# Top-32 attention and a low-rank mixer: first batch's last steps masked at once on VectorE, weight rounding with sign bits from ScalarE

## The chip, the cores and the metric

One core of one Trainium2 chip runs the whole program: one launch, all inputs and outputs in the chip's memory. The metric is the device time of one execution in microseconds. Times of a kernel are medians over several executions; the profile is one more execution, with its own time. The profile's "span" runs from the first to the last recorded instruction of that execution.

Five engines matter. TensorE (PE, with PEld for its weight loads) multiplies matrices and transposes tiles through an identity matrix. VectorE (DVE) finds maxima and masks. ScalarE (ACT) evaluates exponentials, scaled copies and rectifications. GpSimd (POOL) does elementwise work. SyncE (SP) issues transfers. Each works through its own list of instructions in order and waits on semaphores for the others.

## The reference

Attention with a top-32 mask per row feeds a mixer. All sizes are fixed: 8 batches, 8 heads, 576 positions, head size 64.

```
scores = scale * q @ k.T                    # (8, 8, 576, 576)
kth    = 32nd largest score of each row
scores = where(scores >= kth, scores, -1e9)
attn   = exp(scores - rowmax)
attn   = attn / (sum(attn) + 1e-9)
x      = (attn @ v), heads side by side     # (8, 576, 512)

u   = x + (x.T @ U @ V).T                   # U: 576x32, V: 32x576
out = u + relu(u @ w_ch1) @ w_ch2           # w_ch1: 512x2048, w_ch2: 2048x512
```

The four parameters U, V, w_ch1 and w_ch2 come in as 64-bit floats and q, k, v as 32-bit floats. The kernel reads each 64-bit number as two 32-bit words and builds the nearest 32-bit float from them with integer arithmetic.

## The kernel before

**Steps.** Heads are taken in pairs: 4 pairs a batch, 32 in all (g). The rows of a pair are cut into four blocks of 128 rows and one of 64 (t = 0 to 4). One pass of the main loop, with counter n and `g, t = divmod(n, 5)`, is called step n here; there are 160 steps, 20 for each batch. At t = 4 both heads' 64 rows share one tile of 128 rows, so such a step has half the work. Step 18 is the last full block of batch 0, and step 19 is its last half block.

**Inside a step.** `scores` multiplies q by k for a block (L271) and ScalarE copies the result to the tile Ssb (L290 to L292, L281). `front` works on VectorE: the eight largest of each row (MAX8, L317), then three rounds of striking these out (MATCH_REPLACE8, L325) and finding the next eight (L329). The smallest of the fourth eight is the threshold. ScalarE's `nmax` (L321) prepares the row maximum and `weigh` (L297) takes the exponential. The first head of a block is weighed early and then masked on VectorE by one SCALAR_TENSOR_TENSOR (L334) that also sums the row. The second head takes another way: after the threshold is known, GpSimd writes a large negative number where a score is too small (L332) and adds it to the scores (L333), and ScalarE takes the exponential after that, in the next step, summing as it goes. `front` is a Python generator: each `next(here)` writes out the instructions up to its next `yield`, and `next(last, None)` writes the late exponential of the step before.

`turns` transposes the weights block by block on TensorE (L361, L366) with ScalarE copies to PT (L362, L367). `values` multiplies PT with v (L390, L393, and L380 at t = 4), with copies to XT (L402) and at t = 4 the scaled copies to x (L388). At t = 4 it also writes the inverse of the row sums `den` (L377, L378) for all nine columns of the pair. `mixed` transposes XT back (L414), scales by the inverse on GpSimd (L419), multiplies with U (`pT`, L425, copy Tb L433) and V (`up`, L437 and L439) and stores u in uT (L447).

**Feed-forward part.** When a batch's four pairs are mixed, `mlp` becomes a stream of matmuls (L462 with copies hT L474, then L481, adds L497 and output turns L509) that `fill` deals out between the attention instructions in fixed portions. So batch b's feed-forward work runs beside batch b + 1's attention, and batch 7's runs alone at the end. During batch 0 there is nothing to deal out.

**The turn.** ALONE is 20: steps up to 20 are written out by a first branch of the loop and later ones by a second. In step 20 the first branch also finishes values of steps 18 and 19 and all of `mixed` for pair 3, so that the first L462 can follow.

**Rounding of parameters.** 36 groups of 64-bit words are loaded and rounded: four small ones for U and V, 16 blocks of w_ch1, 16 of w_ch2. `next_params(1)` is one turn of a three-stage pipeline: it joins the group that was converted at the previous call (`f64_join`), converts the one that was loaded at the previous call (`f64_parts`) and issues the load of a new one on SP's queue (512 KB for a weight block). The conversion is ScalarE's absolute value (L157), GpSimd's maximum with a tiny number (L158), ScalarE's scaling of the low word's top byte (L159) and ScalarE's sign (L160). The join is VectorE's shift left by three (L168), GpSimd's addition of the sign word (L169) and GpSimd's addition of the low word with its rounding (L171). It is called once a step, and a second time in steps 11 and 16 and, after step 20, where t is 1 or 3.

**Order.** Nothing reorders instructions on TensorE, ScalarE, VectorE and GpSimd: each does them in the order in which the Python code writes them out. So moving a call moves its instructions past everything between.

Of the kernel before, what the change touches and what calls it, by code (L numbers as in the profile page):

```python
# [8 lines left out]
F32 = mybir.dt.float32  # L9
U8 = mybir.dt.uint8  # L10
U32 = mybir.dt.uint32
AF = mybir.ActivationFunctionType
ALU = mybir.AluOpType
# [8 lines left out]
def kernel(  # L22
# [28 lines left out]
    nc = tc.nc  # L51
    B, H, S, D = q.shape
    P = 128
# [51 lines left out]
    V = const.tile([NT * R, S], F32, name="V")  # L105

    step = const.tile([P, 1], F32, name="step")
    nc.vector.memset(step, 2.0**23)
# [32 lines left out]
    def f64_parts(raw, out):  # L141

        n, w = raw.shape[0], raw.shape[-1] // 2
        d = "p f" if len(raw.shape) == 3 else "p"
        low, hi = (raw.rearrange(f"{d} (w two) -> {d} w two", two=2)[..., i] for i in range(2))
        low8 = raw.bitcast(U8).rearrange(f"{d} (w eight) -> {d} w eight", eight=8)[..., 3]
        if out is None:
            if not spare:  # L150

                uT = mlpp.tile([P, NC, S], F32, tag="uT", name="uT")
                words = uT.rearrange("p c n -> p (c n)").bitcast(U32)
                spare.extend(words[:, i * SLAB : (i + 1) * SLAB] for i in range(NT))
            out = spare.pop()[0:n, 0:w]
        bits = out.bitcast(U32)
        nc.scalar.activation(bits.bitcast(F32), hi.bitcast(F32), AF.Abs)  # L157
        nc.gpsimd.tensor_scalar(bits.bitcast(F32), bits.bitcast(F32), TINY, None, ALU.max)  # L158
        nc.scalar.activation(low, low8, AF.Identity, bias=step[0:n], scale=(1 + 2.0**-10) / 32)  # L159
        nc.scalar.activation(hi.bitcast(F32), hi.bitcast(F32), AF.Sign, bias=nudge[0:n])  # L160
        return hi, bits, low

    def f64_join(hi, bits, low, outs):

        nc.vector.tensor_single_scalar(bits, bits, 3, ALU.logical_shift_left)  # L168
        nc.gpsimd.tensor_tensor(bits, bits, hi, ALU.add)  # L169
        for dst, form in outs:  # L170
            nc.gpsimd.tensor_tensor(dst.bitcast(U32), form(bits), form(low), ALU.add)  # L171

# [126 lines left out]
    def front(g, t):  # L299
# [18 lines left out]
        yield  # L318
        for i in range(1, TOPK // 8):
            if i == 1:  # L320
                nc.scalar.mul(nmax[:, 0:n], first[:, 0:n, 0], -SCALE)  # L321
                weigh(chunks[0], Es[0], nmax[:, 0:1])
# [8 lines left out]
        if n == 2:  # L331
            nc.gpsimd.tensor_scalar(Es[1], chunks[1], ms[1][:, 7:8], NEG, ALU.is_lt, ALU.mult)  # L332
            nc.gpsimd.tensor_tensor(chunks[1], chunks[1], Es[1], ALU.add)  # L333
        nc.vector.scalar_tensor_tensor(  # L334
            out=Es[0],
            in0=chunks[0],
            scalar=ms[0][:, 7:8],
            in1=Es[0],
            op0=ALU.is_ge,
            op1=ALU.mult,  # L340
            accum_out=sums[0],
        )
# [3 lines left out]
        if n == 2:  # L346
            weigh(chunks[1], Es[1], nmax[:, 1:2], sums[1])
# [21 lines left out]

    def values(g, t):  # L370
# [4 lines left out]
        if t == NT:  # L375
            den, x = dens[g], xs[g % 2]
            nc.vector.tensor_scalar_add(den, den, 1e-9)  # L377
            nc.vector.reciprocal(den, den)  # L378
# [26 lines left out]
    def mixed(g, wait):  # L405
# [4 lines left out]
        XT, den = XTs.pop(g), dens.pop(g)  # L410
# [144 lines left out]
    t = 0  # L555
# [5 lines left out]
    for n in range(STEPS + 2):  # L561
# [9 lines left out]
        if n <= ALONE:  # L571
            next(turning, None)
            next(turning, None)
            if n < ALONE:
                scores(*divmod(n + 1, CH))
# [3 lines left out]
            if n == ALONE:  # L579

                next(turning)
                next(turning)
# [3 lines left out]
            if n == ALONE:  # L586
                values(*divmod(n - 1, CH))
                mixing.append(mixed((n - 1) // CH, 1))
                fill()
                scores(*divmod(n + 1, CH))  # L590
                while mixing:
                    fill()
            next_params(1)
            if n and n < ALONE:
                next(turning)
# [74 lines left out]
```

## Time and profile before

| what | value |
|---|---|
| median of 3 executions | 1872.28 us (1869.91 to 1872.94) |
| the profiled execution's own time | 1873.04 us |
| its span | 1871.2 us, 29270 instructions |
| PE busy | 1751.0 us, 94% |
| DVE busy | 1620.9 us, 87% |
| ACT busy | 1008.6 us, 54% |
| POOL busy | 690.8 us, 37% |

Busy time by stage, in microseconds, with TensorE's granted clock as a share of full speed:

| stage (us) | PE | DVE | ACT | POOL | clock |
|---|---|---|---|---|---|
| 0 to 240 | 143.33 | 225.44 | 140.23 | 148.17 | 0.71 |
| 240 to 355 | 103.94 | 104.82 | 81.47 | 97.41 | 1.00 |
| 355 to 1735 | 1372.93 | 1287.03 | 768.70 | 444.52 | 1.00 |
| 1735 to 1871 | 130.79 | 3.63 | 18.24 | 0.72 | 0.99 |

The first stage is batch 0's attention with the first 20 joins of parameters. In the second the feed-forward matmuls of batch 0 run beside batch 1's attention and the w_ch2 blocks are rounded. The third has no rounding left. The last is batch 7's feed-forward part alone.

In the listings that follow, a line of a timeline gives start and duration in microseconds, engine, line, operation, tiles written and read, and in brackets the engine's idle time before the instruction with what ended it. A line of the chain gives start, length and what the chain passed through: the chain is followed back from the last instruction, at each step to whatever released it.

### The profile page before, as it was taken

How to read it: one execution, taken by the hardware profiler on the slowest of the kernel's cores; microseconds unless marked ns; L12 is line 12 of the kernel's file. 1: busy time of each engine (PE TensorE's matmuls, PEld its weight loads, DVE VectorE, ACT ScalarE, POOL GpSimd, SP SyncE). 2: the span in 40 equal slices, each digit the busy share in tenths (PEclk: the TensorE clock that was granted, in tenths of full speed). 3: DMA queues.
4: the chain of work that ended last, by engine and by line, in shares of the span. 5: the costliest groups of instructions: out<-in, count | busy, mean ns of one | idle time of the engine just before them, and what ended most of it. 6: DMA issues, size and time to landing. Idle time of an engine off the chain costs nothing.

```text
span 1871.2 us, 29270 instructions
## 1 busy us (share of the span) xinstructions
PE 1751.0 (94%) x10528; PEld 1327.4 (71%) x10528; DVE 1620.9 (87%) x3312; ACT 1008.6 (54%) x2467; POOL 690.8 (37%) x470
## 2 busy tenths in 40 slices
PE   4566699999999999999999999999999999999999
PEld 3344466687677877788777877778777877778777
DVE  7999989999999999999999999999999999996000
ACT  4566576665555555555555556565655655554111
POOL 3667788633223332333323333333233232322000
PEclk7667699999999999999999999999999999999999
DMA  3222222110001010101001010010001010000000
GB/s 86 65 71 74 67 84 80 41 25 23 18 17 31 21 32 20 28 22 26 14 24 30 22 32 19 24 26 20 20 20 31 24 30 21 9 8 7 6 14 12
DMA packets 127296, 58.23 MB, mean 31 GB/s; under 512 B 89904, under 2 KB 124976, under 8 KB 127152
## 3 DMA queue, kind: packets, MB, share of 16 engines
q1 hardware_dynamic: 126096, 56.10, 11.1%
q8 instruction: 84, 1.38, 0.3%
q14 instruction: 60, 0.49, 0.1%
q10 hardware_dynamic: 1056, 0.26, 0.1%
HBM read 46.89 MB, written 9.44 MB: 30 GB/s over the span
## 4 chain that ended last, share of the span: by engine, by line
PE 85%; DVE 7%; ACT 5%; POOL 1%; issue 1%; DMA 0%; POOLq 0%; SPq 0%; DVEq 0%; ACTq 0%
PE mm L462 27%; PE mm L481 25%; PE sc L271 9%; PE O L393 7%; PE tp L361 6%; DVE rr L325 3%; DVE m L329 2%; PE up L437 2%; PE O L380 2%; PE O L390 2%; PE tp L251 1%; ACT E L297 1%; DVE first L317 1%; PE tp L509 1%; PE up L439 1%
## 5 line engine op out<-in xcount | busy, mean ns | idle before, releaser
L329 DVE MAX8 m<-rr 128x8 f32<-128x576 f32 x864 | 614.6, 748 | 5.3
L481 PE MATMUL mm<-hT,w 128*128 128x256 f32 (+1 forms) x2048 | 562.4, 410 | 0.0
L462 PE MATMUL mm<-uT,w 128*128 128x256 f32 (+1 forms) x2048 | 558.2, 411 | 1.5 <-ACT hT L474 1.5
L332 POOL TENSOR_SCALAR E<-Ssb,m 128x576 f32<-128x576 f32 x128 | 287.9, 2249 | 619.5 <-DVE m L329 495.2
L462 PEld LDWEIGHTS mm<-uT,w 128*128 128x128 f32 x2048 | 364.6, 191 | 107.9 <-issue 27.9
L481 PEld LDWEIGHTS mm<-hT,w 128*128 128x128 f32 x2048 | 361.3, 191 | 97.2 <-issue 22.5
L325 DVE MATCH_REPLACE8 rr<-m,rr 128x576 f32<-128x576 f32 x576 | 427.5, 742 | 0.0
L361 PE MATMUL tp<-ident,E 128*128 128x128 f32 x1152 | 185.3, 286 | 59.5 <-ACT E L297 42.1
L362 ACT COPY PT<-tp 128x512 f32<-128x512 f32 x288 | 168.1, 584 | 120.0 <-PE tp L361 118.1
L297 ACT ACTIVATE E<-Ssb,nmax 128x576 f32<-128x576 f32 x288 | 223.8, 777 | 7.6 <-POOL Ssb L333 2.4
L361 PEld LDWEIGHTS tp<-ident,E 128*128 128x128 f32 x1152 | 144.8, 147 | 112.8 <-ACT E L297 54.7
L271 PE MATMUL sc<-qkT 64*128 64x288 f32 (+1 forms) x1280 | 212.3, 453 | 0.2 <-ACT Ssb L292 0.2
L325 DVE MATCH_REPLACE8 rr<-first,Ssb 128x576 f32<-128x576 f32 x288 | 211.7, 742 | 0.0
L317 DVE MAX8 first<-Ssb 128x8 f32<-128x576 f32 x288 | 205.3, 749 | 0.9 <-ACT Ssb L292 0.9
L334 DVE SCALAR_TENSOR_TENSOR E<-Ssb,m,E 128x576 f32<-128x576 f32 x160 | 138.2, 864 | 63.2 <-ACT E L297 46.9
L333 POOL TENSOR_TENSOR Ssb<-Ssb,E 128x576 f32<-128x576 f32 x128 | 180.3, 1409 | 10.7
L474 ACT ACTIVATE hT<-mm 128x320 f32<-128x320 f32 (+1 forms) x256 | 104.2, 407 | 119.9 <-PE mm L462 119.1
L402 ACT COPY XT<-O 128x128 f32<-128x128 f32 x128 | 34.0, 266 | 213.6 <-PE O L393 213.6
L271 PEld LDWEIGHTS sc<-qkT 64*128 64x128 f32 (+1 forms) x1280 | 110.4, 187 | 51.6 <-issue 25.0
L393 PE MATMUL O<-PT,va 128*64 128x128 f32 x2048 | 146.3, 287 | 0.0
L494 DVE TENSOR_TENSOR oT<-uT,mm 128x320 f32<-128x320 f32 (+1 forms) x8 | 3.6, 454 | 146.6 <-PE mm L481 146.6
L393 PEld LDWEIGHTS O<-PT,va 128*64 128x64 f32 x2048 | 114.7, 142 | 16.4 <-issue 2.2
(75 smaller groups left out, 1543.0 us busy)
## 6 DMA issues: line engine op xcount, KB each, us to landing
raw<-in_moe_w_ch_dram SPq DMA_DIRECT2D x32, 512.0 KB, 3.7
va<-in_v_dram SPq DMA_DIRECT2D x64, 128.0 KB, 2.4
out_dram<-ob SPq DMA_DIRECT2D x64, 128.0 KB, 1.9
ld_q<-in_q_dram SPq DMA_DIRECT2D x63, 128.0 KB, 2.7
ld_k<-in_k_dram SPq DMA_DIRECT2D x63, 128.0 KB, 2.8
ld_ends<-in_q_dram SPq DMA_DIRECT2D x32, 32.0 KB, 2.1
ld_ends<-in_k_dram SPq DMA_DIRECT2D x32, 32.0 KB, 2.1
vd<-in_v_dram SPq DMA_DIRECT2D x64, 16.0 KB, 2.0
```

The lines of the kernel that those rows point to most:

```text
L271: nc.tensor.matmul(sc[slice(0, n) if t < NT else half(h), h, 0:HALF], lhsT=qkT[half(h), 0, cols(t)], rhs=qkT[half(h), 1, i * HALF : (i + 1 ...
L297: nc.scalar.activation(E, chunk, AF.Exp, bias=nmax, scale=SCALE, accum_out=total)
L317: nc.vector.max(ms[c], curs[c])
L325: nc.vector.match_replace(nxt, ms[c], curs[c], NEG)
L329: nc.vector.max(ms[c], curs[c])
L332: nc.gpsimd.tensor_scalar(Es[1], chunks[1], ms[1][:, 7:8], NEG, ALU.is_lt, ALU.mult)
L333: nc.gpsimd.tensor_tensor(chunks[1], chunks[1], Es[1], ALU.add)
L361: nc.tensor.transpose(tp[:, j, :], E2[:, a : a + P], ident)
L362: nc.scalar.copy(PT[:, NT * h : NT * h + NT], tp)
L393: nc.tensor.matmul(O[half(h)], lhsT=va[:, h, j, :], rhs=PT[:, NT * h + j], start=False, stop=(j == NT - 1),)
L462: nc.tensor.matmul(ph[:, 0:w], lhsT=w1[:, cc, f * P : (f + 1) * P], rhs=uT[:, cc, lo:hi], start=(cc == 0), stop=(cc == NC - 1),)
L481: nc.tensor.matmul(po[:, 0:w], lhsT=w2[:, f, c * P : (c + 1) * P], rhs=hTs[f][:, 0:w], start=(f == 0), stop=(f == NF - 1),)
```

## The change

It has three parts.

1. **Rounding.** The conversion gets a fourth ScalarE instruction: after the sign, Identity with scale 2^30 and bias -2^30, written as a 32-bit integer, turns +1 into 0 and -1 into the sign bit alone. The join's shift on VectorE and the sign's addition on GpSimd become one VectorE instruction with two tensor inputs (shift left by three, then exclusive or). The constants change to suit. For each of the 36 groups ScalarE has one instruction more, GpSimd one less, and VectorE's has one input more.
2. **Step 18.** Both heads are weighed early and masked on VectorE; nothing of this step goes to GpSimd.
3. **Steps 19 and 20.** They get a branch of their own. Step 19 writes out all remaining turns of step 17, the scores of step 20, all turns of step 18, the values of 17 and 18, the inverse of the first eight row sums and the first part of `mixed` for pair 3; it has no call of `next_params`. Step 20 writes out the turns and values of 19 (with the inverse of the ninth row sum), the multiplication with U, then the scores of 21 and the rest of `mixed`. The later parameter groups each move one call back.

```diff
-        nc.scalar.activation(low, low8, AF.Identity, bias=step[0:n], scale=(1 + 2.0**-10) / 32)
+        lows = low.bitcast(F32)
+        nc.scalar.activation(lows, low8, AF.Identity, bias=two[0:n], scale=(1 + 2.0**-10) * 2.0**-27)
         nc.scalar.activation(hi.bitcast(F32), hi.bitcast(F32), AF.Sign, bias=nudge[0:n])
+        nc.scalar.activation(hi.bitcast(I32), hi.bitcast(F32), AF.Identity, bias=less[0:n], scale=2.0**30)
         return hi, bits, low
...
-        nc.vector.tensor_single_scalar(bits, bits, 3, ALU.logical_shift_left)
-        nc.gpsimd.tensor_tensor(bits, bits, hi, ALU.add)
+        nc.vector.scalar_tensor_tensor(
+            out=bits, in0=bits, scalar=3, in1=hi, op0=ALU.logical_shift_left, op1=ALU.bitwise_xor
+        )
...
+        pooled = n == 2 and (g, t) != (NPAIR - 1, NT - 1)
...
-                weigh(chunks[0], Es[0], nmax[:, 0:1])
+                for c in range(1 if pooled else n):
+                    weigh(chunks[c], Es[c], nmax[:, c : c + 1])
...
-        if n == 2:
+        if pooled:
             nc.gpsimd.tensor_scalar(Es[1], chunks[1], ms[1][:, 7:8], NEG, ALU.is_lt, ALU.mult)
             nc.gpsimd.tensor_tensor(chunks[1], chunks[1], Es[1], ALU.add)
-        nc.vector.scalar_tensor_tensor(
+        for c in range(1 if pooled else n):
+            nc.vector.scalar_tensor_tensor(
...
-        if n == 2:
+        if pooled:
             weigh(chunks[1], Es[1], nmax[:, 1:2], sums[1])
...
+    def inverse(g, lo, hi):
+        den = dens[g][:, lo:hi]
+        nc.vector.tensor_scalar_add(den, den, 1e-9)
+        nc.vector.reciprocal(den, den)
...
-            nc.vector.tensor_scalar_add(den, den, 1e-9)
-            nc.vector.reciprocal(den, den)
+            inverse(g, 2 * NT if g == NPAIR - 1 else 0, 2 * NT + 1)
...
+        if n >= ALONE - 1 and n <= ALONE:
+
+            list(turning)
+            if n < ALONE:
+                scores(*divmod(n + 1, CH))
+            list(turns(*divmod(n - 1, CH)))
+            if n < ALONE:
+                values(*divmod(n - 2, CH))
+                next(here)
+            values(*divmod(n - 1, CH))
+            if n < ALONE:
+                inverse(g, 0, 2 * NT)
+                next(here)
+                mixing.append(mixed(g, 1))
+                fill()
+                next(here)
+                next(here)
+                continue
+            fill()
+            scores(*divmod(n + 1, CH))
+            next(here)
+            while mixing:
+                fill()
+            next_params(1)
+            fill()
+            next(last, None)
+            next(here)
+            fill()
+            next(here)
+            next(here)
+            fill()
+            continue
```

In the first branch of the loop, now for steps below 19 alone, the lines for step 20 are gone; the calls of the other steps stay as they were.

## The prediction

> **What bounds the kernel now.** I read the page first (slices, then the chain), then the chain, the engine timelines and the busy times for the first 480 us, which is where the change lies. Step n below is pass n of the main loop; E(n) is its score tile after the mask.
>
> The slices show two regimes. Up to about 240 us VectorE is at nine tenths and TensorE at half of a reduced clock; afterwards TensorE is full.
>
> ```profile
> PE   4566699999999999999999999999999999999999
> DVE  7999989999999999999999999999999999996000
> PEclk7667699999999999999999999999999999999999
> ```
>
> From 11 to 241 us VectorE has one gap (0.48 us at 217.42), so the attention steps 0 to 19 run at VectorE's pace. From 239 to 355 us the feed-forward matmuls of batch 0 run beside the steps, and there VectorE's share misleads. The chain for this stretch contains no VectorE piece. It alternates between TensorE and ScalarE, and the three weight-rounding instructions (L157, L159, L160) lie on it, ahead of the copies and the exponentials that TensorE waits for:
>
> ```profile
> 270.57 0.78 ACT E L297
> 271.35 0.57 ACT w L157
> 271.91 0.67 ACT raw L159
> 272.59 0.66 ACT raw L160
> 273.24 0.02 issue
> 273.27 0.44 ACT hT L474
> 273.70 0.48 ACT PT L362
> 274.18 0.76 ACT E L297 x2
> ```
>
> TensorE's timeline shows the matching gaps, in brackets with their releaser:
>
> ```profile
> 273.76 0.81 PE L462 MATMUL mm<-uT,w 128*128 128x320 f32 x2 [0.81 <-ACT hT L474]
> ...
> 285.43 0.66 PE L361 MATMUL tp<-ident,E 128*128 128x128 f32 x4 [1.54 <-ACT E L297]
> ...
> 332.15 0.66 PE L361 MATMUL tp<-ident,E 128*128 128x128 f32 x4 [1.80 <-ACT E L297]
> ```
>
> VectorE in the same stretch waits six times (8.4 us) for the rounding maximum on GpSimd; that is its slack against this loop. From 355 to the end TensorE has one larger gap (2.9 us at 470, behind GpSimd's mask of that step), so whatever the loop loses by 355 stays in the span.
>
> **The change, part by part.**
>
> *Rounding on VectorE.* L168 is one-input; its successor starts 0.33 us later (220.56 to 220.88). The two-input form has no row. Bounds: unchanged rate (+0) below; above, the mask L334, 0.82 us with its successor after 0.74, so +0.41. The nearest rows for 512 values at one per cycle are VectorE's copies L253 (512 values, 0.69) and L290 (576, 0.76); less the 0.07 by which neighbours overlap (a pair of maxima takes 1.41 for two of 0.75) that gives 0.62, so I take +0.30. Seventeen of the twenty joins up to step 18 have this width: 17 x 0.30 = 5.1, and 0.1 for the small ones.
>
> *GpSimd loses L169* (1.29 to 1.46 us, 36 times). What it gives VectorE is less collision:
>
> ```profile
> 204.03 1.76 DVE L334 SCALAR_TENSOR_TENSOR E<-Ssb,m,E 128x576 f32<-128x576 f32 x1
> 209.83 1.30 DVE L168 TENSOR_SCALAR w<-w 128x512 uint32<-128x512 uint32 x1
> 224.27 0.82 DVE L334 SCALAR_TENSOR_TENSOR E<-Ssb,m,E 128x576 f32<-128x576 f32 x1
> ```
>
> The first stood against GpSimd's L171 (203.89 to 205.18), the second against L333 (209.43 to 210.84), which was late behind the rounding. There are four such in stage one (148.86, 154.66, 204.03, 209.83), 0.88 to 0.94 each. I take 3.0 saved, with 0 and 3.6 as ends.
>
> The Trainium skill (SBUF — State Buffer, Who interferes with whom) says that a VectorE instruction with two SBUF inputs contends with any GpSimd instruction that reads SBUF, and that the later one fully blocks. The trace agrees for GpSimd's tensor-tensor but not for its tensor-scalar: the third line above took 0.82 with L158 running from 223.72 to 225.22. By the rule's wording a join that meets the 1.5 us L158 would wait too and the rounding would cost up to 1.5 us more at each meeting; by the row it costs nothing, and the sum goes by the row.
>
> *Step 18.* Its second head is masked on VectorE: +0.82 by L334. So E(18) ends 5.2 - 3.0 + 0.8 = 3.0 us later (ends: -2.8 and +7.9). Off GpSimd go 2.2 + 1.4 us (L332, L333).
>
> *The turn from step 18 to the feed-forward part.* Before, E(18)'s VectorE mask ended at 218.16, the second head came through GpSimd and a late exponential only at 225.0, and the first L462 started at 239.05: 20.9 us. After, I walk the changed kernel's order of instructions on TensorE. The scores of step 20 end 0.75 after E(18): they ended at 218.28 against 218.16, and ScalarE now has a second exponential (0.69) and a conversion (0.66) ahead of the one they wait behind, against the mask's 0.8 on the other side. Then transposes of 18: 2.4; values of 17 and 18: 2.6 each; wait and XT transposes 1.2; transposes of 19: 1.4; PT copy 0.6; values of 19: 2.4; L388 0.65; pT 0.7; scores of 21: 1.25; up 1.75. That is 18.3 us at the durations of this stage, whose clock is low. In the trace the clock came up after some 8 us without a gap (scores 2.29 us at 215.99, 1.24 at 234.46). TensorE now has fewer gaps, so it may come up from values(18) on, which takes 3.3 off: 15.0. I take the middle, 16.6. So L462 starts 3.0 - 4.3 = 1.3 us earlier than 239.05. The split inverse costs VectorE two small instructions in step 19 (0.15 and 0.21, the rows of L377 and L378 at 229.12), and the join dropped there gives back 0.33.
>
> *The added ScalarE conversion*, the one that decides. No row has it; the rows of the same width with a bias operand, L159 and L160, have pitches of 0.65 to 0.67. The ends are L157's 0.57 and L159's whole 0.77; I take 0.66, since form and bias are theirs. On a stretch where ScalarE runs without a gap from the score copies to the instruction TensorE waits for, it lengthens the loop by all of it. Before, fourteen conversions follow 239 us; after, fifteen, since step 19 no longer makes one and all later ones move one place back. Step by step: step 20, nothing (TensorE has 5.4 us of L462 queued); 21, 0.66 and 0.05 (its second conversion has 0.6 of cover before L390); 22, 0.66 (gap of 0.65 at 262.44); 23, twice 0.66 (gaps at 273.76 and 277.87); 24, 0.66; 25, 0.22 (hT has 0.43 of cover); 26, 0.4 (Tb waits for the two conversions, while pT gains from GpSimd's missing L169); 27, 0.66; 28, twice 0.66; 29, 0.66; 30, 0.15 (the displaced one, beside a TensorE that has no gap). Nine full ones are 5.9, the rest 0.8: 6.7 us. If only half bite: 3.4; if every one bites and the displaced one wholly (2.5): 12.
>
> The Trainium skill (ScalarE: Activation LUTs, Rules for kernel authors and What ACT_TABLE_LOAD costs) speaks against the move: additions and multiplications belong on VectorE. Its price for 512 values with a pointer bias is 0.28 + 0.43 - 0.09 = 0.61 us per successor, so 9 x 0.61 = 5.5 as an estimate by that page where the rows give 5.9.
>
> *Costed at nothing.* VectorE after 240 us: sixteen joins at +0.30 are 4.8, covered by the 8.4 us that it waits. If that cover goes, it sets the pace instead (rival two). The dropped call in step 19 also moves a 512 KB load one place back in SP's queue, behind the next pair's V; it lands in 3.7 us and is converted a step (some 11 us) later. The last weight block is joined in step 31 rather than 30, near 359; its first reader, a late L481 of that step, ran at 365.1. That leaves 6 us.
>
> **Sum.** -1.3 + 6.7 = +5.4 on the span: 1871.2 + 5.4 = 1876.6. The profiled execution took 1873.04, 1.84 more than its span: 1878.4. It was 0.76 above the median of 1872.28, so the forecast is 1877.7.
>
> **Rivals.**
> *One: the loop has more give than its gaps say.* For it: TensorE starts the loop some 4 us further ahead of VectorE, and waits that belong to VectorE leave room. Against: the brackets name ScalarE, which was itself without a gap. Half of the conversions bite and the clock comes up early: 3.0 - 5.9 + 3.4 = +0.5, 1872.8.
> *Two, faster: VectorE is the clock to 470 us*, as its 95% says, and the change frees it. Its waits of 8.4 go; collisions saved come to 5.0 over both stages; 33 joins cost 9.9 and the mask 0.8: -2.7, and the 0.8 that L334 waits at 443 goes too: 1868.8. It decides as soon as the loop's own path falls below that -3.5: if L462 starts 5 us earlier, say, and no more than two conversions bite. Against: no VectorE piece is in the chain from 239 to 443.
> *Three: dearer joins.* At +0.41 and with no collision saved, E(18) is 7.9 late, L462 starts 3.6 late, and the loop adds 6.7: +10.3, 1882.6. For it: the raw words are read with a stride. Against: GpSimd's L169 on the same stride takes 1.29, no more than its dense L333 (1.41 for 576).
>
> **How the numbers follow.** The forecast's case 0.55, rival one 0.23, rival two 0.11, rival three 0.11. The likeliest case's own range is 1874 to 1881. The range takes in rival one, a little below it for an early start, and three: 1871.8 to 1882.7. Differences under 0.2% (3.7 us) can't be told from none in this kernel. Of the forecast's case a fifth lies below that line, and a fifth of rival one above it: slower 0.44 + 0.05 + 0.11 = 0.60; faster 0.10, nearly all of rival two; within, the rest, 0.30.
>
> **What would show it.** In the new profile: joins with a successor after 0.62; fewer masks of 1.76 before 220; the first feed-forward matmul near 238 and E(18)'s two masks back to back; a fourth ScalarE rounding instruction of 0.66 on the chain nine times or so between 240 and 355; VectorE's waits for the rounding maximum nearly gone but replaced by waits for scores or exponentials; TensorE full after some 359. I am wrong if VectorE fills that chain, if L462 starts far from 238, or if TensorE's gaps between 240 and 355 don't grow over their 11 us.

## The result and the profile after

The changed kernel took 1879.44 us (median of 4, 1877.60 to 1881.03) against 1872.61 (4, 1869.91 to 1873.62) for the kernel before: a ratio of 1.0038, 95% interval 1.0021 to 1.0056. It is slower by 6.8 us, which is more than the 0.2% that can be told from none. The profiled execution took 1879.65 us with a span of 1877.8, 6.6 us more than the span before.

The line numbers have moved: feed-forward matmuls L474 (were L462) and L493 (L481), copies hT L486 (L474), transposes of E L369 (L361), exponential L302 (L297), masks L342 (L334), and in the rounding L160 absolute value, L161 maximum, L163 low byte, L164 sign, the new L165, join L172, last addition L176. Three places in the trace divide the difference: the first feed-forward matmul, the last `pT` before TensorE is full (step 31), and the end. An instruction's end is taken as the start of the next on its engine.

| from, to (us) | before | after | difference |
|---|---|---|---|
| start of the span to the end of E(18) on VectorE | 218.16 | 218.42 | +0.3 |
| from there to the first feed-forward matmul | 20.89 | 14.55 | -6.3 |
| from there to the `pT` of step 31 (361.83, now 368.68) | 122.78 | 135.71 | +12.9 |
| from there to the end of the span | 1509.4 | 1509.1 | -0.3 |

The `pT` of step 31, before and then after:

```profile
361.83 0.62 PE L425 MATMUL pT<-x,U 128*32 128x128 f32 x10
368.68 0.62 PE L437 MATMUL pT<-x,U 128*32 128x128 f32 x10
```

So the turn gained about six microseconds, and the loop after it lost twice that. The page's slices, of 47 us each, show both:

```profile
PE   4556788899999999999999999999999999999999
DVE  7999999899999999999999999999999999996000
PEclk7667799999999999999999999999999999999999
```

In the fifth slice (188 to 235 us) TensorE's share and clock are 7 where both were 6; in the sixth to eighth (235 to 376) TensorE's share is 8 where it was 9.

**The start.** VectorE's timeline after shows the two masks of step 18 back to back, with no idle time shown before them:

```profile
216.94 0.82 DVE L342 SCALAR_TENSOR_TENSOR E<-Ssb,m,E 128x576 f32<-128x576 f32 x1
...
217.68 0.81 DVE L342 SCALAR_TENSOR_TENSOR E<-Ssb,m,E 128x576 f32<-128x576 f32 x1
```

None of the masks of 1.76 us is left before 220.

**The turn.** TensorE's timeline before has a second idle time of 3.8 us, in which the late exponential of step 18 was awaited, and slow matmuls behind it:

```profile
225.17 1.12 PE L361 MATMUL tp<-ident,E 128*128 128x128 f32 x4 [3.79 <-ACT E L297]
...
229.47 1.98 PE L393 MATMUL O<-PT,va 128*64 128x128 f32 x16
...
239.05 2.32 PE L462 MATMUL mm<-uT,w 128*128 128x320 f32 x8
```

After, that idle time is gone, and the same sixteen matmuls take 1.09 instead of 1.98 us from 223 us on:

```profile
216.54 1.11 PE L369 MATMUL tp<-ident,E 128*128 128x128 f32 x4 [5.12 <-ACT E L302]
...
223.00 1.09 PE L405 MATMUL O<-PT,va 128*64 128x128 f32 x16
...
232.97 5.55 PE L474 MATMUL mm<-uT,w 128*128 128x320 f32 x20
```

Granted clock before: 0.50 from 224 to 234 us. After: 0.50 from 215 to 222 us, and 1.00 from there to 273. The turn's gain is the waiting that is gone and the faster matmuls behind it.

**The loop.** The chain of waits (start, length, what it passed through) after, in the step whose lines were shown of before. The four rounding instructions stand between the exponential and the copies that TensorE waits for:

```profile
266.90 0.78 ACT E L302
267.68 0.58 ACT w L160
268.26 0.65 ACT raw L163
268.92 0.66 ACT raw L164
269.60 0.76 ACT raw L165
270.38 0.44 ACT hT L486
270.82 0.48 ACT PT L370
271.29 0.78 ACT E L302 x2
```

The fourth is dearer than its neighbours: in ScalarE's own timeline L164 starts 0.67 after L163 (268.14 to 268.81), but L165 starts 0.79 after L164 (269.60), whose result it reads. From the start of L160 to the first instruction that is not the rounding's, a conversion now keeps ScalarE for 2.70 us (median of the 14 from 238 to 360 us) where it kept it for 1.89: 0.81 more, not 0.66. L165 is on the chain twelve times between 240 and 360 us. Seven of TensorE's ten gaps have grown by about that amount (here 0.81 to 1.59, 1.54 to 2.35, 1.80 to 2.58):

```profile
270.87 0.81 PE L474 MATMUL mm<-uT,w 128*128 128x320 f32 x2 [1.59 <-ACT hT L486]
...
284.37 0.66 PE L369 MATMUL tp<-ident,E 128*128 128x128 f32 x4 [2.35 <-ACT E L302]
...
336.49 0.66 PE L369 MATMUL tp<-ident,E 128*128 128x128 f32 x4 [2.58 <-ACT E L302]
```

In the loop (from the first feed-forward matmul to step 31) TensorE's idle times in brackets sum to 10.9 us before and 17.1 after. There is a second loss: instructions that ran longer than the median of their own form add 1.0 us before and 6.4 after. TensorE's granted clock was 0.50 for 13.7 us of this loop, behind three of the gaps; in the kernel before it never fell there. The busy times of three stretches of 3 us after (columns PE, PEld, DVE, ACT, POOL, then the clock as a share of full speed) show one of them:

```profile
303.00:306.00 3.00, 1.01 (x8) 0.42 (x10) 2.85 (x4) 2.97 (x7) 1.92 (x3) 1.00 0.12 34
306.00:309.00 3.00, 2.45 (x17) 1.56 (x18) 3.00 (x8) 2.97 (x6) 3.00 (x2) 0.67 0.05 11
309.00:312.00 3.00, 3.00 (x9) 2.11 (x10) 2.96 (x7) 0.66 (x2) 2.92 (x3) 0.50 0.50 164
```

How the 12.9 us come together can be read from conversion to conversion: the time from the start of one (its absolute value on ScalarE) to the start of the next, after less before. The first of the 14 stretches, from the conversion of step 20, grew by nothing. Eight grew by 0.77 to 0.84 each, one (step 25) by 0.55. The three in which the clock fell grew by 1.03, 2.48 and 1.38, which is 2.5 more than three times 0.8. The last, up to the `pT` of step 31, grew by 1.13; it holds the conversion that the change moved back.

VectorE no longer waits mostly for the rounding maximum (8.4 us in all before, 240 to 480 us), but for ScalarE's exponentials:

```profile
DVE E L342 <- ACT E L302: 5.4, 4, 3.0
DVE w L172 <- POOL w L161: 3.5, 2, 3.2
DVE E L342 <- PE tp L369: 1.6, 1, 1.6
```

### The profile page after: what moved, and what is told of

It is laid out like the page before. It is cut to its first block, busy times and chain, and to the rows that moved or that the text cites. A ratio compares the mean times of both kernels' runs of the same rounds, so it can differ in the third digit from the quotient of the medians.

```text
span 1877.8 us, 29298 instructions
## 1 busy us (share of the span) xinstructions
PE 1750.1 (93%) x10528; PEld 1322.9 (70%) x10528; DVE 1623.7 (86%) x3317; ACT 1034.9 (55%) x2502; POOL 642.3 (34%) x432
## 3 DMA queue, kind: packets, MB, share of 16 engines
q1 hardware_dynamic: 126096, 56.10, 11.2%
q8 instruction: 84, 1.38, 0.3%
## 4 chain that ended last, share of the span: by engine, by line
PE 85%; ACT 7%; DVE 6%; issue 1%; POOL 1%; DMA 0%; POOLq 0%; SPq 0%; DVEq 0%; ACTq 0%
PE mm L474 26%; PE mm L493 26%; PE sc L276 9%; PE O L405 7%; PE tp L369 6%; DVE rr L332 2%; DVE m L336 2%; PE up L449 2%; PE O L392 2%; PE O L402 2%; ACT E L302 1%; PE tp L256 1%; PE up L451 1%; PE tp L521 1%; PE tp L374 1%
## 5 line engine op out<-in xcount | busy, mean ns | idle before, releaser
L493 PE MATMUL mm<-hT,w 128*128 128x256 f32 (+1 forms) x2048 | 564.6, 411 | 0.0
L474 PE MATMUL mm<-uT,w 128*128 128x256 f32 (+1 forms) x2048 | 559.2, 411 | 3.3 <-ACT hT L486 3.3
L474 PEld LDWEIGHTS mm<-uT,w 128*128 128x128 f32 x2048 | 363.9, 190 | 110.8 <-issue 28.3
L493 PEld LDWEIGHTS mm<-hT,w 128*128 128x128 f32 x2048 | 361.5, 191 | 98.1 <-issue 23.3
L332 DVE MATCH_REPLACE8 rr<-m,rr 128x576 f32<-128x576 f32 x576 | 427.7, 742 | 0.0
L369 PE MATMUL tp<-ident,E 128*128 128x128 f32 x1152 | 184.8, 285 | 63.1 <-ACT E L302 49.4
L369 PEld LDWEIGHTS tp<-ident,E 128*128 128x128 f32 x1152 | 144.8, 147 | 116.1 <-ACT E L302 61.6
L302 ACT ACTIVATE E<-Ssb,nmax 128x576 f32<-128x576 f32 x288 | 223.7, 777 | 5.2
L332 DVE MATCH_REPLACE8 rr<-first,Ssb 128x576 f32<-128x576 f32 x288 | 211.8, 742 | 0.0
L342 DVE SCALAR_TENSOR_TENSOR E<-Ssb,m,E 128x576 f32<-128x576 f32 x161 | 137.0, 852 | 70.7 <-ACT E L302 52.9
L486 ACT ACTIVATE hT<-mm 128x320 f32<-128x320 f32 (+1 forms) x256 | 104.4, 408 | 119.2 <-PE mm L474 118.5
```

The source lines that it names most:

```text
L302: nc.scalar.activation(E, chunk, AF.Exp, bias=nmax, scale=SCALE, accum_out=total)
L332: nc.vector.match_replace(nxt, ms[c], curs[c], NEG)
L369: nc.tensor.transpose(tp[:, j, :], E2[:, a : a + P], ident)
L474: nc.tensor.matmul(ph[:, 0:w], lhsT=w1[:, cc, f * P : (f + 1) * P], rhs=uT[:, cc, lo:hi], start=(cc == 0), stop=(cc == NC - 1),)
L493: nc.tensor.matmul(po[:, 0:w], lhsT=w2[:, f, c * P : (c + 1) * P], rhs=hTs[f][:, 0:w], start=(f == 0), stop=(f == NF - 1),)
```

## The experiments

Theory L: the time lost is ScalarE's, because every instruction added to a conversion lies on the loop between ScalarE and TensorE. Rival V: VectorE's join with two inputs costs it. Rival T: the turn or the dropped call does. In all runs "first" is the start of the first feed-forward matmul, "loop" the way from there to the `pT` of step 31, and "conversion" the median time that one keeps ScalarE in the loop, all from the profiled execution; the ratio is of means, to the kernel before on the same chip, with its 95% interval. A profile is one execution, and "first" varies from one to the next: h_dup_late, which has the code of before up to step 20, has it 1.6 us earlier. It is 237.46 to 241.41 in the four kernels with the old turn, and 231.99 to 235.80 in the eight with the new turn that have no rounding call in step 19.

| run | time | ratio | first | loop | conversion |
|---|---|---|---|---|---|
| before | 1872.15 to 1872.61 | 1 | 239.05 | 122.78 | 1.89 |
| after | 1879.44 | 1.0038 [1.0021, 1.0056] | 232.97 | 135.71 | 2.70 |
| a_turn | 1869.37 | 0.9985 [0.9977, 0.9994] | 232.12 | 127.67 | 1.90 |
| b_round | 1885.18 | 1.0071 [1.0058, 1.0085] | 241.41 | 134.23 | 2.69 |
| c_onesign | 1868.79 | 0.9984 [0.9975, 0.9993] | 232.96 | 124.88 | 1.89 |
| d_reorder | 1879.65 | 1.0038 [1.0026, 1.0051] | 235.80 | 135.11 | 2.7 |
| f_turn_keep19 | 1871.05 | 0.9992 [0.9984, 1.0001] | 235.24 | 125.05 | |
| l_turn_order | 1869.50 | 0.9989 [0.9980, 0.9998] | 231.99 | 126.72 | |
| h_dup_late | 1880.18 | 1.0055 [1.0041, 1.0069] | 237.46 | 132.06 | 2.59 |
| g_dup_early | 1874.09 | 1.0009 [1.0000, 1.0018] | 239.10 | 122.76 | |
| n_lowpool | 1874.49 | 1.0013 [1.0005, 1.0022] | 233.86 | 128.12 | 2.23 |
| r_lowpool_fp8sign | 1869.78 | 0.9993 [0.9984, 1.0002] | 233.03 | 125.93 | 1.31 |
| s_oldjoin | 1871.33 | 0.9999 [0.9990, 1.0008] | 232.97 | 126.57 | 1.31 |

**The two halves of the change, each alone.** The first run has the new turn and step 18 with the old rounding; the second the new rounding in the old order of steps.

```diff
 a_turn, against the changed kernel
-        nc.scalar.activation(hi.bitcast(I32), hi.bitcast(F32), AF.Identity, bias=less[0:n], scale=2.0**30)
...
-        nc.vector.scalar_tensor_tensor(
-            out=bits, in0=bits, scalar=3, in1=hi, op0=ALU.logical_shift_left, op1=ALU.bitwise_xor
-        )
+        nc.vector.tensor_single_scalar(bits, bits, 3, ALU.logical_shift_left)
+        nc.gpsimd.tensor_tensor(bits, bits, hi, ALU.add)
```

> The changed kernel with the rounding of the kernel before: only step 18's masks and the new branch for steps 19 and 20 remain of the change. Theory L (the loop between TensorE and ScalarE from 240 to 355 us sets the time there, and every ScalarE instruction on it counts): the first L462 moves from 239.05 to about 233.5, the loop grows only by the one conversion that moves behind the turn (1.9 us), so the span falls by about 3.8 us, to a median near 1868.8. Rival V (VectorE sets the pace to 470 us): it has only one mask more than before, +0.7, and gains nothing from an early start of the matmuls: 1872 to 1873.5. Rival T (the new branch, with the weight groups one call later, is what costs): 1877 or more.

> The kernel before with the new rounding alone (fourth ScalarE instruction, one VectorE join with two inputs, no sign addition on GpSimd); steps 18 to 20 as before. Theory L: stage one is even (joins +4.5, collisions about -5), L462 starts near 238.5, and fourteen conversions at 0.81 us each (0.67 of its own and 0.14 because the new instruction waits for the sign's result) add 11.3: about +10.8, a median near 1883.4. Rival V: the joins cost 33 x 0.26 = 8.6, collisions and waits saved give 8 to 13 back: 1868 to 1873. Rival T: about as before, 1872.6.

They came at 1869.37 and 1885.18: the halves have opposite signs, and the rounding alone is slower than the whole change. Rivals V and T fall. The loop of the rounding alone is 11.45 us longer than before, close to fourteen conversions of 0.80 more (11.2). But the equality is in part chance: from conversion to conversion nine of the fourteen stretches grew by 0.75 to 0.81 and one by 0.54, two by nothing, and the two in which the clock fell by 2.45 and 1.42. The turn alone brings the first matmul forward by 6.9 us, but the end by only 2.8 (1.1 to 4.3 by the interval): its loop grew by 4.9 us, where theory L had 1.9 for the conversion that moves.

**One ScalarE instruction for two.** The join on VectorE stays; the sign and the new conversion become one instruction. The weights get other signs than the reference's, so this run stands for time alone.

```diff
-    nc.vector.memset(less, -(2.0**30))
+    nc.vector.memset(less, -0.0)
...
-        nc.scalar.activation(hi.bitcast(F32), hi.bitcast(F32), AF.Sign, bias=nudge[0:n])
-        nc.scalar.activation(hi.bitcast(I32), hi.bitcast(F32), AF.Identity, bias=less[0:n], scale=2.0**30)
+        nc.scalar.activation(hi.bitcast(F32), hi.bitcast(F32), AF.Identity, bias=less[0:n], scale=0.0)
```

> The changed kernel with the two ScalarE sign instructions replaced by one: the high word times 0.0 plus -0.0, whose result is a zero with the word's sign. It leaves out the nudge that makes very small negative words positive. ScalarE has as many instructions a conversion as before; VectorE's two-input join and GpSimd's saving stay. Theory L: start of L474 near 232.5, loop longer only by the displaced conversion (1.9): -4 or so against before, a median near 1868.5. Rival V: as the changed kernel, 1879, since the joins are the same. Rival T: also 1878 or more.

1868.79: 10.7 us go with this one instruction, and the loop is 10.8 us shorter than after, again about 14 x 0.81 = 11.3. VectorE's joins are those of after, so V falls. Eight of TensorE's gaps are those of before to 0.04 us; two of them (0.81 and 1.80 before):

```profile
267.67 0.81 PE L473 MATMUL mm<-uT,w 128*128 128x320 f32 x2 [0.81 <-ACT hT L485]
...
328.16 0.66 PE L368 MATMUL tp<-ident,E 128*128 128x128 f32 x4 [1.82 <-ACT E L301]
```

**Another order of the four.** The sign is issued ahead of the low byte, so that L165 no longer follows the instruction whose result it reads.

```diff
+        nc.scalar.activation(hi.bitcast(F32), hi.bitcast(F32), AF.Sign, bias=nudge[0:n])
         lows = low.bitcast(F32)
         nc.scalar.activation(lows, low8, AF.Identity, bias=two[0:n], scale=(1 + 2.0**-10) * 2.0**-27)
-        nc.scalar.activation(hi.bitcast(F32), hi.bitcast(F32), AF.Sign, bias=nudge[0:n])
```

> The changed kernel with the order of a conversion's ScalarE instructions changed to absolute value, sign, low byte, sign bits, so that the new instruction no longer directly follows the one whose result it reads. Theory L: the wait of about 0.14 us before the new instruction goes, fifteen times on the loop: -2 against the changed kernel, about 1877.4; in the profile the pitch from sign to the next falls from 0.80 to 0.66. Rivals V and T: no difference, 1879.4.

A miss: 1879.65, as after. L165 now follows its predecessor after 0.65 us, as expected, but the sign follows the absolute value after 0.72, where the low byte followed it after 0.57 (medians), and the conversion still takes 2.7. The time that I took for a removable wait only moved to another pair.

**A ScalarE instruction where the change is not.** The kernel before, with the absolute value issued twice: in one run in the conversions of step 20 and later, in the other in those before 20.

```diff
         nc.scalar.activation(bits.bitcast(F32), hi.bitcast(F32), AF.Abs)
+        if at_step[0] >= 20:
+            nc.scalar.activation(bits.bitcast(F32), hi.bitcast(F32), AF.Abs)
```

> The kernel before, with the rounding's first ScalarE instruction (absolute value) issued twice in the fourteen conversions of steps 20 and later, none other changed. Theory L (any ScalarE instruction added to a conversion in the loop from 240 to 355 us lies on the path): 14 x 0.57 = 8.0 us, up to 11 if TensorE's granted clock falls in the longer gaps: 1880 to 1883. Rival V (VectorE's two-input join is what cost the time): no join is changed, so 1872.2. Rival half (only half of them bite): 1876.

> The kernel before, with the rounding's first ScalarE instruction issued twice in the conversions of the steps before 20, none after. Theory L: ScalarE is at two thirds there and VectorE sets the pace, so nothing but the conversions near the turn can be seen: 0 to +1.5 us, 1872.2 to 1873.7. Rival (ScalarE is on the path of stage one as well): 0.57 us for each of the twenty conversions, +11, 1883.

Late: 1880.18 (the ratio is larger than this median says, as two of five executions took 1884 and 1886), and the loop 9.3 us longer for fourteen conversions of 0.70 more (9.8). From conversion to conversion the first stretch grew by nothing and the other thirteen by 0.42 to 1.08. Nothing of the change is in this kernel, and its gaps are nearly those of after (1.46 and 2.29 beside 1.59 and 2.35):

```profile
274.93 0.81 PE L464 MATMUL mm<-uT,w 128*128 128x320 f32 x2 [1.46 <-ACT hT L476]
...
288.27 0.65 PE L363 MATMUL tp<-ident,E 128*128 128x128 f32 x4 [2.29 <-ACT E L299]
```

Early: first matmul, loop and `pT` of step 31 within 0.05 us of before. The time is 1.8 us above it (interval 0 to 3.4), none of it at the places that the edit touches; I leave it open. So the price of a ScalarE instruction depends on the stage: nothing that shows in the 20 steps in which VectorE sets the pace, nearly all of it in the loop after.

**Why the turn's gain does not arrive.** Two more versions of the turn with the old rounding: one keeps the rounding call in step 19, the other puts GpSimd's addition to x ahead of the rounding in the step where TensorE's `pT` had waited 2.55 us for it.

```diff
 f_turn_keep19, in step 19
                 inverse(g, 0, 2 * NT)
                 next(here)
+                next_params(1)
...
 l_turn_order, in the second branch
-        next_params(1)
         if n - 2 >= ALONE and (n - 2) % CH == NT:
             mixing.append(mixed((n - 2) // CH, 4))
-        fill()
+            fill()
+            next_params(1)
+        else:
+            next_params(1)
+            fill()
```

> Turn and step 18 of the change with the old rounding, as in the run that gave 1869.4, but step 19 keeps its rounding call, so one conversion fewer (three ScalarE instructions, 1.9 us) falls after 240 us and one more before. Theory L (each conversion after 240 us lies whole on the ScalarE-TensorE loop): the way from the first feed-forward matmul to the last pT before 355-365 us shrinks from 127.7 to about 125.8 us; the first feed-forward matmul comes 0 to 1.9 us later than 232.1; time 1867.5 to 1869.4. Rival T (the call in step 19 stands in the way of the turn and costs it whole, and the loop has that much give): first matmul at 234, no gain in the loop, 1871.3.

> Turn of the change with the old rounding, and in the two steps where a pair's mixing starts, its first part (GpSimd's addition to x among it) is issued ahead of the rounding call instead of behind it. Theory O (what is left of the early start is lost because pT waits for GpSimd's addition behind the rounding work, 2.55 us at step 26): that gap goes to under 0.6, the last pT of the loop comes about 2 us earlier (near 357.8), time 1867.4. Theory L alone (ScalarE is the pace again one step later): the gap moves to the next E or hT wait and the time stays at 1869.4.

Keeping the call shortens the loop by 2.6 and delays the first matmul by 3.1: neither theory whole, and no gain. Nor is the moved conversion what the turn alone loses: in a_turn the last stretch, which holds it, is as long as before. That kernel loses its 4.9 us nearly all in two stretches, 3.1 from 275 to 289 us and 1.7 from 302 to 315, where `pT` waits 2.55 us and the clock falls. In the first TensorE waits 2.97 us, up to 280.09, for a late exponential, and the chain of a_turn there is GpSimd's, rounding and then masking:

```profile
270.90 1.74 POOL w L169
...
272.71 1.29 POOL w L171
274.00 1.45 POOL w L159
275.45 2.20 POOL E L334
...
277.74 1.41 POOL Ssb L335
```

Its first instruction starts at 270.89. It reads the result of a shift that VectorE, without a gap since 217 us, ended at 270.75; the profile names a ScalarE copy to PT, which ended with it, as what it waited for. Which of the two held it is not decided. The other order takes the gap ahead of `pT` away, as theory O said, and the `pT` of step 31 comes 1.1 us earlier, but the time stays at 1869.5, as theory L alone said: VectorE's wait for the rounding maximum on GpSimd rose from 5.6 to 7.2 us instead. An expected gain that turned into another wait.

**Less on ScalarE than before.** The low byte goes to GpSimd; then the sign bit is also made by one ScalarE instruction; then the old join comes back.

```diff
 n_lowpool, against the changed kernel
-        nc.scalar.activation(lows, low8, AF.Identity, bias=two[0:n], scale=(1 + 2.0**-10) * 2.0**-27)
+        nc.gpsimd.tensor_scalar(lows, low8, (1 + 2.0**-10) * 2.0**-27, 2.0, ALU.mult, ALU.add)
...
 r_lowpool_fp8sign, besides
-        raw = mlpp.tile([P, 2 * C], U32, tag="raw", name="raw", bufs=3)
+        raw = mlpp.tile([P, 2 * C], U32, tag="raw", name="raw", bufs=2)
...
-        nc.scalar.activation(hi.bitcast(F32), hi.bitcast(F32), AF.Sign, bias=nudge[0:n])
-        nc.scalar.activation(hi.bitcast(I32), hi.bitcast(F32), AF.Identity, bias=less[0:n], scale=2.0**30)
+        nc.scalar.activation(tops, hi.bitcast(F32), AF.Identity, bias=zero[0:n], scale=2.0**-30, saturate=False)
...
 s_oldjoin, besides
-        nc.vector.scalar_tensor_tensor(
-            out=bits, in0=bits, scalar=3, in1=hi, op0=ALU.logical_shift_left, op1=ALU.bitwise_xor
-        )
+        nc.vector.tensor_single_scalar(bits, bits, 3, ALU.logical_shift_left)
+        nc.gpsimd.tensor_tensor(bits, bits, hi, ALU.add)
```

(`tops` is the top byte of each word of a zeroed tile, seen as an 8-bit float; the tile is the join's second input. To make room for two such tiles, the raw words have two buffers for three in this run and the next.)

> The changed kernel, with the conversion of the low byte (multiply and add) moved from ScalarE to GpSimd, so a rounding has three ScalarE instructions again, and GpSimd three (about 1.5 us more each time, which brings it back to what it did before the change). Theory L (a ScalarE instruction more or less in the loop is what counts, whichever it is): like the run with one sign instruction, first feed-forward matmul near 233, from there to the last pT of the loop some 125 us, 1868.8. Rival P (GpSimd's queue takes ScalarE's place: pT and the joins wait for it): at least the changed kernel's gaps ahead of pT grow by 1.5 each and the time stays at 1874 or more.

> As the run before it, and the sign bit made by one ScalarE instruction: a value scaled to nothing and written as an 8-bit float (0x80 or 0x00) into the top byte of a zeroed word; a rounding has two ScalarE instructions, one fewer than before the change. The raw words have two buffers for three, to make room. Theory L, if the loop stays ScalarE's: 14 x 0.67 = 9 us less than the run before it: 1860. Rival V (with one sign instruction VectorE waited only 1.1 us in all from 240 to 480 us, so there VectorE is already the clock): 1 to 2 us less, 1867 to 1868.

> As the run with two ScalarE instructions, but the join is the old one again: a one-input shift on VectorE and the sign added by GpSimd. In that run VectorE's pieces fill the chain from 235 to 330 us. Theory V (there VectorE's two-input join is now on the path): its pitch falls by 0.26, 14 x 0.26 = 3.6 us from the loop: 1866. Rival P (GpSimd takes VectorE's place: 1.3 us more for it ahead of each rounding maximum, two of which lie on that chain already, and its two-input additions block masks again): 1870 to 1873.

n_lowpool came at 1874.49, 5.0 below after and 5.7 above what L gave. Its three instructions are not the three of before: a conversion takes 2.23, because the sign and the one that reads it stand next to each other. 14 x 0.34 = 4.8 of that is more than c_onesign's, and the loop is 3.2 longer. From conversion to conversion eleven of its stretches are 0.27 to 0.39 longer than c_onesign's. So it is the time on ScalarE that counts, not the number of instructions. The time is within what P gave, but P's sign is absent: the gap ahead of `pT` fell from 1.99 to 1.51 where P had it grow by 1.5, and most of the gaps that grew over c_onesign's (1.18 for 0.82, 1.09 for 0.81, 2.08 for 1.82) name ScalarE. GpSimd took 0.66 us for the low byte, not the 1.5 that I had taken from its maximum.

r_lowpool_fp8sign has the shortest conversion, 1.31, 0.58 below c_onesign's. By L alone that is 8.1 us. The loop did not get shorter, 125.93 against 124.88, and the time is 1869.78. Rival V holds here. VectorE waits for 2.0 us in all from 240 to 480, and the chain from 290 to 310 us, where before had only TensorE, ScalarE and GpSimd, is VectorE alone (some of it):

```profile
304.60 0.82 DVE E L351 x2
305.42 1.32 DVE first L331 x2
306.74 1.46 DVE rr L341 x2
...
308.78 0.74 DVE m L345
309.53 0.59 DVE w L181
```

The two buffers cost something too: ScalarE now waits three times, 5.0 us in all from 235 to 362, for raw words to land, which none of before, after, c_onesign and n_lowpool does there. These waits are not on the chain from 235 to 330 us, but no run here has this conversion and three buffers.

s_oldjoin takes the second input off VectorE again and gives GpSimd the addition: 1871.33, VectorE waits 4.6 us for the maximum on GpSimd. That is the time of rival P, and the 0.26 saved at each join does not arrive. But how much a later GpSimd takes is open, for the two buffers act as well: two loads behind GpSimd's additions stand on the chain, 3.40 us at 245.20 and 3.56 at 269.51, and ScalarE waits 8.8 us for raw words.

```profile
243.88 1.30 POOL w L184
...
245.20 3.40 DMA raw<-in_moe_w_ch_dram
248.62 0.67 ACT w L164
```

None of these beats the kernel before by 0.2%. The best with the right signs is a_turn: 0.9985 [0.9977, 0.9994].

## Why the prediction came out as it did

The forecast was 1877.7, the changed kernel took 1879.44; on the span 1876.6 against 1877.8. The direction, the place and the mechanism were those of the forecast, but its sum is -1.3 + 6.7 where the trace has -6.1 + 12.9. Two terms were off, by 4.8 and by 6.2 us in opposite directions. So the mechanism was forecast, but that the number came within 1.7 us is luck.

*Rounding on VectorE: the row was right, +0.30 became +0.26.* A join of 0.67 has a successor after 0.59 (139.41 to 140.00 us). 17 x 0.26 = 4.4 for 5.1.

*GpSimd's collisions: mis-sized.* The forecast took 3.0 of at most 3.6, from four masks and joins. Seven are gone by the trace: the four named (148.86, 154.66, 204.03, 209.83: 0.88 to 0.94 each), the addition to the row sums at 182.36 (1.11 where it takes 0.15 alone), and two smaller ones at 84.47 and 179.96 (0.26 and 0.32): 5.2 in all. I had looked for masks and joins of double length only. The two smaller ones also limit the reading that GpSimd's tensor-scalar does not hold a mask up: they stood beside L332, which is one. With the second mask's 0.74 that makes 4.4 + 0.7 - 5.2 = -0.1. E(18) ended 0.3 later, not 3.0; the 0.4 between the two I did not trace.

*The turn: the working was right, the choice of the middle was not.* The forecast had 18.3 at a slow clock and 15.0 if the clock came up early, and took 16.6. It took 14.55. The row that decides was in TensorE's timeline: the 3.79 us of idle time that ended at 225.17 stand at the start of the slow stretch, and the change takes away what they waited for. I had seen that there would be fewer gaps, and did not ask whether one was left that could lower the clock. Nor does the clock need "some 8 us without a gap": before, it rose at 234.19, 5.4 us after the last gap had ended at 228.75. Together the start is 6.1 earlier, not 1.3.

*The added conversion: right in place, half the size.* The term was 6.7 and measured 12.9. Three steps failed, and the stretches from conversion to conversion size them. The price: 0.66 came from rows of instructions that don't read their neighbour's result; L165 reads L164's, and the conversion grew by 0.81. On the nine that were priced in full that is 1.2 us. The cover: the second conversion of step 21, that of step 25 and the two of step 26 were priced low by holding each against TensorE's idle time at that place before (0.05, 0.22 and 0.4 for two). They cost 0.79, 0.55 and, without the clock, 1.6: 2.3 more. Where ScalarE runs without a pause from one step to the next, a delay that TensorE has cover for in this step is still there in the next. The one of step 20, behind 5.4 us of queued matmuls, cost nothing, as said. Third, the clock: it fell three times in the longer gaps, 2.5 us that no term foresaw. The remaining 0.2 lie in the last stretch. So the total is near the upper end that the prediction gave ("if every one bites", 12), but not for its reason: the moved conversion, which was to add 2.5 there, cost 0.4 at most. b_round gives 11.45 for fourteen, c_onesign takes 10.8 off again, h_dup_late 9.3 for fourteen of 0.70; each of these sums holds some clock as well.

*Costed at nothing.* VectorE's joins after 240 us were covered, as said: no VectorE piece is on the chain of the changed kernel from 240 to 355 us, and c_onesign, which has all the two-input joins, is no slower than a_turn, which has none. The moved load and the last weight block did not show: from 349 to 473 us TensorE has no gap.

*Rival one* (half of the conversions bite) falls by b_round and h_dup_late. *Rival three* (dearer joins) falls by the 0.26. *Rival two* (VectorE is the clock) was wrong for the change, but its condition was the best number in the text: it decides "as soon as the loop's own path falls below that -3.5", which puts the `pT` of step 31 at 358.3. With the new turn and a conversion of 1.9 or less, six kernels have it at 357.84, 358.71, 358.96, 359.54, 359.79 and 360.29: one below that, the others at most 2.0 above, whatever else is taken off ScalarE or moved. In the two at or below 359 that have the new join (c_onesign, r_lowpool_fp8sign) VectorE waits no more than 2.0 us from 240 to 480, and 58 and 68% of the chain from 240 to 355 is VectorE's. There VectorE is the clock. With the old join and a conversion of 1.9 it is not: the chain of a_turn and l_turn_order has no VectorE piece from 240 to 355 us, and VectorE waits 5.6 and 7.2 us for GpSimd's maximum. GpSimd's rounding and masking is on that chain where most of the turn's gain is lost, and so the 6.9 us arrive as 2.8.

*What would show it.* Joins with a successor after 0.59 (said: 0.62), no slow mask before 220, first matmul at 232.97 (said: near 238; "far from 238" was a sign of being wrong, and for the turn it was), a fourth instruction on the chain twelve times (said: nine), waits for the maximum down from 8.4 to 3.5 and replaced by waits for exponentials, gaps grown from 11 to 17: five of six as written, in kind.

## What to carry to other kernels

Where an engine runs without a pause through many steps and lies on the loop, price an added instruction at its full time in every step: cover seen at one wait is used once, not in every step. Take the price from a neighbour that stands in the same relation to its predecessor (reads its result, writes over its words), not only from one of the same shape. And ask for every gain how soon the next engine becomes the clock: here ScalarE's time was paid nearly in full down to the old conversion's 1.9 us. Below it r_lowpool_fp8sign gained nothing, as VectorE had been only 3.5 us behind. And longer gaps can cost clock on top: look where each falls, as the next section shows.

## What the runs showed of the hardware

*TensorE's clock is set stretch by stretch, not gap by gap.* In each of the thirteen traces all changes of the granted clock lie whole multiples of 3.413 us apart, to 4 ns. From 239 to 1735 us it fell 29 times from 1.00 to 0.50, and TensorE had been busy for 16 to 46% of the stretch of 3.41 us just before. Every stretch at full clock with less than 41% was followed by a fall, none with more than 46% was. So a gap counts by how it lies on this grid. After, 1.59 and 0.44 us (up to 270.87 and 272.11) fall into one stretch and leave it 46% busy; the 2.35 us up to 284.37 are divided between two:

```profile
269.47:272.88 3.41, 1.57 (x8) 0.99 (x9) 3.38 (x7) 3.35 (x8) 0.87 (x2) 1.00 0.20 69
272.88:276.29 3.41, 3.41 (x9) 1.94 (x7) 3.03 (x8) 3.10 (x7) 3.41 (x3) 0.50 0.28 78
...
279.71:283.12 3.41, 2.31 (x10) 1.32 (x8) 2.68 (x6) 3.38 (x6) 3.38 (x3) 1.00 0.25 71
283.12:286.53 3.41, 2.16 (x11) 1.70 (x12) 3.41 (x8) 2.38 (x6) 0.01 (x1) 1.00 0.24 83
```

Likewise before's 2.56 us up to 306.98 are divided at 305.87 and lower nothing, and after's 2.58 us up to 336.49, which lie almost wholly in one stretch (36% busy), lower the clock. The Trainium skill (TensorE: Matmul & The Clock Gate, Part 1: The HAM clock gate) puts the fall behind an idle window of about 3.4 us that runs freely. The length of the window and its fixed grid agree with these traces; that it must be idle does not, since 46% busy was little enough.

*Two ScalarE instructions of which the second reads the first's result* don't follow each other at the 0.66 us of independent ones: in ScalarE's timeline of n_lowpool the sign begins 0.70 after the absolute value, and L165 begins 0.81 after the sign, with no idle time shown.

```profile
267.08 0.67 ACT L160 ACTIVATE w<-raw 128x512 f32<-128x512 f32 x1
267.78 0.78 ACT L164 ACTIVATE raw<-raw,nudge 128x512 f32<-128x512 f32 x1
268.59 0.76 ACT L165 ACTIVATE raw<-raw,less 128x512 int32<-128x512 f32 x1
```

Medians over the conversions of a run show two cases. Behind the sign, an instruction that reads its result starts after 0.79 to 0.81 us, another after 0.67. Behind the absolute value, one that writes over the words which that read or wrote starts after 0.70 to 0.72 (n_lowpool, d_reorder, h_dup_late); one that writes elsewhere starts after 0.57, also where it reads the same words (r_lowpool_fp8sign). Why is not shown.

*GpSimd took less for bytes*: a multiplication and addition of 128 x 512 bytes took 0.66 us, its maximum of 128 x 512 floats 1.49. The operations differ too, so this does not single out the type.
